# Interleaved memory attention and token-mixing MLP: weights streamed in row blocks over two head groups

## The chip, the cores and the metric

The kernel runs on one core of a Trainium2 chip. The metric is the device time of one execution in microseconds (us), as the median of the runs shown. PE is the matrix engine, DVE the vector engine, ACT the scalar engine, POOL the GpSimd engine; SP issues most of the transfers, and 16 DMA engines carry them out.

## What is computed

Two layers A and B are applied in turn, twice, each on a layer norm of x (2048 tokens, 640 features, bf16) and with a residual. A is an attention with a recurrent memory, cut to what matters:

```python
mem = mem0                                     # 8 rows of 640
for s in range(64):                            # segments of 32 tokens
    h = concat([mem, x[32*s:32*s+32]])         # 40 rows
    q, k, v = h @ Wq, h @ Wk, h @ Wv           # 32 heads of 192: weights 640 x 6144 each
    p = softmax(where(mask, q @ k.T * scale, -1e9))
    o = (p @ v) @ Wo                           # 6144 x 640
    mem = o[:8]; outs.append(o[8:])            # the next segment needs this one's memory
```

B is a token mixer and an MLP: `h = gelu(layernorm(x) @ w1)`, then the four quarters of the 640 features of h are shifted by +1, -1, +2 and -2 tokens, `x1 = x + shifted @ w2`, and the result is `x1 + gelu(layernorm(x1) @ w3) @ w4` with 1536 inner features.

## The kernel before

**Steps and lanes.** The recurrence makes A serial in its segments. The kernel runs the first A layer (lane 0) and the second (lane 1, five segments behind, `LAG`) side by side: one call of `attention_step(t)` computes segment t of lane 0 and segment t - 5 of lane 1, 2 x 40 = 80 columns. There are 69 steps; the first five and the last five have one lane only (40 columns). Every step needs all weights of A (4 x 7.86 MB), which do not fit on the chip, so a part stays resident and the rest is streamed again in every step.

**Attention.** Heads go in 8 groups of 4 (`HG`). `proj(g)` computes keys and queries feature-major (weights stationary, the 80 columns of `hT` moving, L503, 30 matmuls each) and copies them to `kT` (DVE) and `qT` (ACT). Values are made token-major (the columns of `hT` stationary, 384 weight columns moving, L535, two halves of 5 matmuls) and copied by ACT (L540). `attend(g)` has scores (L558), mask and minimum (L569), four exponentials, one a head, each with its row sum (L577), the reciprocal (L582) and the product (L583) on DVE, transposes of the probabilities (L591) and their copy (L596), the product with the values (L605), its copy `oT` (L611), and the output product into `psy` (L623). The output products of the last three groups are due at the step's end (`OT_BUFS` is 4). `psy` gives the memory columns of the next step's `hT` (L640), on which all of its projections wait.

**Weights.** Each of the four weights has 8 x 2 units of half a group; a unit of Wq, Wk or Wv is 640 x 384, loaded by one DMA with rows of 768 B, a unit of Wo 384 x 640 with rows of 1280 B; both are 480 KB. Of 64 units `N_RES` = 37 are resident and 27 are streamed in each step through a ring of `RING_A` = 5 slots (tile `wst`, L427).

**Mixer.** Every second step a chunk of 128 rows (64 tokens of both lanes) goes through B in `chunk` and `chunk_end`: transposes (`psx` L783), layer norms, w1 (L873), `gelu`, w2 (L896), w3 in four parts (L928), `gelu`, w4 (L948), and the normalised result (`psn`) goes into lane 1's `hT` (L982). The memory of lane 0's tokens is thus ready some two steps later, which `LAG` covers. Its weights are streamed for each chunk in 12 loads through a ring of `RING_B` = 1 slot (tile `wstB`, `load_b`); w1 comes from a copy `w1d` in device memory that is reordered at the start, and the second load of w2 is five DMAs (L457, L460).

**Order.** Every operation is added to a `Plan` with its engine, a planned duration, a due time (`STEP` = 48 us per step) and the buffers that it reads and writes. `place()` then plays the program through once with these costs and a simple model of the DMAs, and the order that results on each engine is the program. Loads of the two rings are two queues ("wa", "wb"), each in order of due time, and both are issued by SP:

```python
srv = max(s + 1.6, srv) + o.dma / DMA_RATE
done = srv + 0.4
```

PSUM has 8 banks: one for `psy`, three for projections ("P"), two for attention ("S"), two for the mixer ("B").

## Time and profile before

| | |
|---|---|
| median of 3 runs | 4157.51 us (4153.1 to 4164.62) |
| span of the profiled execution | 4200.0 us |
| PE busy | 3679.9 us (88%) |
| DVE busy | 2221.0 us (53%) |
| ACT busy | 1960.1 us (47%) |
| moved by DMA | 1154.32 MB, mean 275 GB/s |

The profiled execution is one of its own and a little longer than the median. Busy times overlap, and matmuls are pipelined, so PE's busy time is an upper reading of its work. A wait is the idle time of an engine ahead of an instruction, put down to what released it; "DMA wstB" is the landing of a load into that tile. The clock is the share of TensorE's 2.4 GHz that was granted; it has two levels, 0.5 and 1.0.

### The profile page before, as it was taken

To read this page: it belongs to the slowest core of one execution; us is meant where nothing else is said; L and a number is where in the kernel's file an instruction comes from. 1 tells how busy PE (TensorE), PEld (TensorE's weight loads), DVE (VectorE), ACT (ScalarE), POOL (GpSimd) and SP (SyncE) were. 2 spreads that over 40 slices of the span, in tenths; PEclk is the share of its full clock that TensorE was granted. 3 is DMA by queue.
4 is the path that set the end of the run, shared out by engine and by line. 5 is a ranking of instruction groups with operands and counts; after the bars stand their busy time and mean duration, and the time that the engine had idled before them with its cause. 6 is when DMAs were issued, how large, how long until landed. Compare 5 with 4: busy or idle time off the path is not lost.

```text
span 4200.0 us, 162257 instructions
## 1 busy us (share of the span) xinstructions
PE 3679.9 (88%) x70351; PEld 3232.6 (77%) x70351; DVE 2221.0 (53%) x6403; ACT 1960.1 (47%) x7380; POOL 280.8 (7%) x489
## 2 busy tenths in 40 slices
PE   6998888889899898989898989888989888989993
PEld 4777877888888787878887888787878777877771
DVE  2455555555555555555555555555545555555452
ACT  2444444444454444544444544444544444445440
POOL 1000000000000000000000000000000000000000
PEclk7999999999999999999999999999999999999995
DMA  9998888888898888988888888888888888889992
GB/s 360 300 312 280 266 267 274 276 281 267 269 289 274 267 277 275 284 273 276 279 271 271 279 273 275 278 263 274 276 254 279 273 275 278 268 280 289 318 298 78
DMA packets 1365962, 1154.32 MB, mean 275 GB/s; under 512 B 44094, under 2 KB 1362380, under 8 KB 1365248
## 3 DMA queue, kind: packets, MB, share of 16 engines
q1 hardware_dynamic: 1357536, 1129.19, 86.0%
q0 software_dynamic: 7712, 14.76, 1.0%
q8 instruction: 552, 9.04, 0.8%
q14 instruction: 162, 1.33, 0.1%
HBM read 1137.72 MB, written 6.06 MB: 272 GB/s over the span
## 4 chain that ended last, share of the span: by engine, by line
PE 67%; DMA 25%; issue 2%; SPq 2%; ACT 2%; DVE 1%; POOL 0%; ACTq 0%; POOLq 0%; DVEq 0%
DMA wstB<-in_B_w_dram 19%; PE psv L535 16%; PE psk L503 13%; PE psq L503 12%; PE psy L623 8%; DMA wstB<-w1d 4%; PE psh L928 3%; PE y L948 3%; PE pso L605 3%; PE pss L558 3%; PE pst L591 2%; PE psh L873 1%; PE hs L896 1%; SPq L460 1%; ACT Pm L577 1%
## 5 line engine op out<-in xcount | busy, mean ns | idle before, releaser
L577 ACT ACTIVATE Pm<-pss,sm 80x80 bf16<-80x80 f32 (+1 forms) x2208 | 673.3, 314 | 186.8 <-DVE sm L569 186.2
L540 ACT CAST V<-psv 80x384 bf16<-80x384 f32 (+1 forms) x1104 | 522.1, 474 | 507.4 <-PE psv L535 504.2
L535 PEld LDWEIGHTS <-hT 128*80 128x80 bf16 (+1 forms) x5520 | 586.4, 117 | 213.7 <-issue 15.8
L503 PEld LDWEIGHTS <-wst 128*128 128x128 bf16 x14490 | 611.3, 103 | 24.8 <-issue 5.9
L535 PE MATMUL psv<-wv,hT 128*80 128x384 bf16 (+1 forms) x3105 | 611.5, 332 | 2.3 <-DMA wv<-in_A_Wv_dram 2.1
L611 DVE CAST oT<-pso 128x480 bf16<-128x480 f32 (+1 forms) x552 | 342.3, 620 | 412.9 <-PE pso L605 411.5
L510 ACT CAST qT<-psq 128x480 bf16<-128x480 f32 (+1 forms) x552 | 292.1, 529 | 504.4 <-PE psq L503 493.9
L535 PE MATMUL psv<-wst,hT 128*80 128x384 bf16 (+1 forms) x2415 | 483.6, 332 | 0.7 <-DMA wst<-in_A_Wv_dram 0.4
L503 PE MATMUL psk<-hT,wk 128*128 128x80 bf16 (+1 forms) x9315 | 441.8, 205 | 17.6 <-ACT hT L640 13.0
L623 PE MATMUL psy<-oT,wo 128*128 128x80 bf16 (+1 forms) x10350 | 454.1, 200 | 2.2 <-DVE oT L611 1.5
L503 PE MATMUL psq<-hT,wq 128*128 128x80 bf16 (+1 forms) x9315 | 440.5, 203 | 5.8 <-DMA wq<-in_A_Wq_dram 5.7
L577 ACT ACTIVATION_READ_ACCUMULATOR Pm<-pss,sm 80x1 f32 (+1 forms) x2208 | 437.0, 198 | 0.0
L503 PEld LDWEIGHTS <-wk 128*128 128x128 bf16 x9315 | 396.8, 104 | 40.4 <-issue 22.2
L569 DVE CUSTOM_DVE_ANT_1 pss<-pss,mask 80x320 f32<-80x320 f32 x472 | 232.8, 493 | 358.5 <-PE pss L558 357.8
L623 PEld LDWEIGHTS <-wo 128*128 128x128 bf16 x10350 | 402.1, 100 | 14.7 <-issue 7.9
L596 ACT COPY PT<-pst 80x320 bf16<-80x320 bf16 (+1 forms) x552 | 221.5, 401 | 369.1 <-PE pst L591 365.3
L518 DVE CAST kT<-psk 128x320 bf16<-128x320 f32 (+1 forms) x552 | 256.3, 464 | 246.5 <-PE psk L503 243.6
L503 PEld LDWEIGHTS <-wq 128*128 128x128 bf16 x9315 | 379.0, 102 | 7.2 <-DMA wq<-in_A_Wq_dram 6.7
L503 PE MATMUL psk<-hT,wst 128*128 128x80 bf16 (+1 forms) x7245 | 357.1, 206 | 2.7 <-DMA wst<-in_A_Wk_dram 2.6
L503 PE MATMUL psq<-hT,wst 128*128 128x80 bf16 (+1 forms) x7245 | 342.4, 203 | 4.4 <-DMA wst<-in_A_Wq_dram 4.4
L524 DVE CAST kT<-psk 64x160 bf16<-64x160 f32 (+1 forms) x1104 | 336.7, 305 | 8.3
L623 PE MATMUL psy<-oT,wst 128*128 128x80 bf16 (+1 forms) x6210 | 284.0, 199 | 53.0 <-DVE oT L611 52.0
(114 smaller groups left out, 4193.2 us busy)
## 6 DMA issues: line engine op xcount, KB each, us to landing
wst<-in_A_Wk_dram SPq DMA_DIRECT2D x483, 480.0 KB, 5.3
wst<-in_A_Wq_dram SPq DMA_DIRECT2D x483, 480.0 KB, 5.5
wst<-in_A_Wv_dram SPq DMA_DIRECT2D x483, 480.0 KB, 5.2
wst<-in_A_Wo_dram SPq DMA_DIRECT2D x414, 480.0 KB, 5.5
wstB<-in_B_w_dram SPq DMA_DIRECT2D x315, 480.0 KB, 4.8
wstB<-w1d SPq DMA_DIRECT2D x35, 480.0 KB, 4.8
wstB<-w1d SPq DMA_DIRECT2D x35, 320.0 KB, 5.2
wstB<-in_B_w_dram SPq DMA_DIRECT2D x35, 160.0 KB, 3.8
```

The costliest lines, as they stand in the source:

```text
L503: nc.tensor.matmul(out=o[:, hf * GCH + cc, 0:N], lhsT=w[:, kc, cc * P:(cc + 1) * P], rhs=h[:, kc, c0:c0 + N], start=(kc == 0), stop=(kc == ...
L510: nc.scalar.copy(out=q[:, :, 0:N], in_=T(pq)[:, :, 0:N])
L518: nc.vector.tensor_copy(out=k4[:, :, 0::3, 0:N], in_=p4[:, :, 0::2, 0:N])
L524: nc.vector.tensor_copy(out=k4[r0:r1, :, j, 0:N], in_=p4[r0:r1, :, 1, 0:N])
L535: nc.tensor.matmul(out=o[0:N, :], lhsT=h[:, kc, c0:c0 + N], rhs=w[:, kc, :], start=(kc == 0), stop=(kc == KC - 1))
L540: nc.scalar.copy(out=v_runs(V_, hf)[0:N], in_=T(pv)[0:N, :].rearrange("n (a b) -> n a b", a=2))
L558: nc.tensor.matmul(out=o[0:N, i * N:(i + w_) * N].rearrange("p (a b) -> p a b", a=w_), lhsT=q[:, c, 0:N], rhs=k_[:, j:j + w_, 0:N], start= ...
L569: nc.vector.tensor_tensor_reduce(out=o, in0=o, in1=maskt[:].unsqueeze(1).to_broadcast([N, HG, N]), scale=-scale, scalar=3.0e38, op0=ALU.ad ...
L577: nc.scalar.activation(out=Pb[0:N, i, 0:N], in_=o[0:N, i * N:(i + 1) * N], func=ACT.Exp, bias=sm_[0:N, 0:1], scale=-1.0, accum_out=sm_[0:N ...
L596: nc.scalar.copy(out=Pt[0:N, :, 0:N], in_=T(pst)[0:N, :, 0:N])
L611: nc.vector.tensor_copy(out=o_[:, :, 0:N], in_=T(pso)[:, :, 0:N])
L623: nc.tensor.matmul(out=o[:, m, c0:c0 + N], lhsT=w[:, cc, m * P:(m + 1) * P], rhs=o_[:, hf * GCH + cc, 0:N], start=st, stop=True, skip_grou ...
```

## The change

- **Row blocks over two groups.** `proj_pair(pr)` takes two head groups at once. A streamed block is 128 rows of Wk, Wq or Wv by 1536 columns (3 KB of each row, 384 KB), and both groups use it. Of the five row blocks of each weight, three are streamed for keys and queries and two for values (`STREAM`); the others are resident. That makes 8 streamed blocks per pair, 32 per step, in a ring of 7 slots of 384 KB. Each group's projection is cut into one operation for the resident rows and one for each streamed block.
- **Wo resident.** All of Wo stays on the chip. Output products of four groups, not three, are due at the step's end.
- **Values feature-major.** Values are computed like keys and queries (30 matmuls a group), copied to `vF` (ACT), transposed on PE (6 a group, `pvt`), and copied to `V` in two halves, one on ACT and one on DVE. `V` has two buffers, not three.
- **Softmax.** One exponential over the four heads, without row sums; DVE adds them up (`tensor_reduce`).
- **Mixer.** w1 and w3 are loaded by rows (w3 in two column halves), at most two row blocks to a load: 3 + 3 + 6 + 6 = 18 loads per chunk in two slots of 384 KB. All output columns of w1, or of half of w3, collect in the two banks at once, and their `gelu`s follow. `w1d` is gone, w2 is loaded in plain rows, and the token shift is made as `gelu` writes `hTB`, in nine pieces, not six.
- **Shared buffers.** `vx` and `xo` are now `vb`; `uw`, `vx2` and `h2T` share `h2u`; there is one `gl`. Projections and attention share one pool of 5 PSUM banks ("A").
- **Planner.** Planned DMA costs are other ones: 380 GB/s, 0.37 us to issue, 2.0 us of latency.

```diff
 HG = 4
-N_RES = 37
-RING_A = 5
-RING_B = 1
+STREAM = {"k": 3, "q": 3, "v": 2}
+RING_A = 7
+RING_B = 2
 STEP = 48.0
-PSUM_POOLS = {"y": 1, "P": 3, "S": 2, "B": 2}
-OT_BUFS = 4
-V_BUFS = 3
+PSUM_POOLS = {"y": 1, "A": 5, "B": 2}
+OT_BUFS = 5
 LAT = 0.2
 PE_LAT = 0.25
-DMA_RATE = 350.0e3
+DMA_RATE = 380.0e3
+DMA_ISSUE = 0.37
+DMA_LAT = 2.0
+LEAD_A = 0.0
+LEAD_B = 0.0
 
...
             cand[e].remove(o)
             out.append(o)
             left -= 1
@@ -246,11 +249,11 @@
...
-    uw = ctile([XB, Dm], f32, "uw")
+    h2u = ctile([P, FC * XB], bf16, "h2u")
+    uw = h2u[:, 0:2 * Dm].bitcast(f32)
+    vx2 = h2u[:, 0:Dm]
+    h2T = h2u[:].rearrange("p (c n) -> p c n", c=FC)
...
+    vx = vb
+    xo = vb
...
-    gl = [ctile([P, 3 * XB], f32, f"gl{i}") for i in range(2)]
+    gl = ctile([P, 3 * XB], f32, "gl")
...
+    ALIAS = {("vx",): ("vb",), ("xo",): ("vb",), ("vx2",): ("uw",)}
...
+    def load_pair(kind, pr, due, now):
+
+        nres = KC - STREAM[kind]
+        cols = slice(PW * pr, PW * (pr + 1))
+        rb, rt = res_tile((kind, pr), [P, nres, PW], w_src[kind][:, 0:nres, cols], due)
+        slots = []
+        for j, kc in enumerate(range(nres, KC)):
+            b = Slotted("ra", None)
+            b.make = lambda b=b: wring.tile([P, SLOT], bf16, name="wst", tag=f"ra{b.slot}")
+
+            def fn(op, b=b, kc=kc):
+                nc.sync.dma_start(out=T(b)[:, 0:PW], in_=w_src[kind][:, kc, cols])
+            add("SP", DMA_ISSUE, due - now + 0.01 * j, fn, w=(b,), dma=2 * P * PW, queue="wa")
+            slots.append(b)
+
+        def view(kc, c0, c1):
+            if kc < nres:
+                return rt[:, kc, c0:c1]
+            return T(slots[kc - nres])[:, c0:c1]
+        return (rb, *slots), view
...
+    def load_b(nm, a, e, due, half=0):
...
+        W = GW if nm == "w3" else Dm
...
-            t = T(b)
...
             if nm == "w1":
-                nc.sync.dma_start(out=v, in_=w1d[:, :, a * P:e * P])
+                nc.sync.dma_start(out=v, in_=w1_v[:, a:e, :])
             elif nm == "w3":
-                nc.sync.dma_start(out=v, in_=w3_v[:, :, a * P:e * P])
+                nc.sync.dma_start(out=v, in_=w3_v[:, a:e, GW * half:GW * (half + 1)])
             elif nm == "w4":
...
-                    for gi in range(4):
-                        nc.sync.dma_start(out=v[32 * gi:32 * gi + 32, 4 - a, :], in_=src[P:QD, gi, :])
-        add("SP", 0.06 if nm != "w2" or e <= 4 else 0.3, due, fn, r=rd, w=(b,), dma=P * n * Dm * 2, queue="wb")
+                nc.sync.dma_start(out=v, in_=w2_v[:, a:e, :])
+        add("SP", DMA_ISSUE, due - LEAD_B, fn, w=(b,), dma=P * n * W * 2, queue="wb")
...
-                        k4 = k_[:].rearrange("p (h c) n -> p h c n", h=2)
-                        nc.vector.tensor_copy(out=k4[:, :, 0::3, 0:N], in_=p4[:, :, 0::2, 0:N])
-                    add("DVE", dve_us(4 * N), s0 + off, fk, r=(pq,), w=(B("kT", G % 2, 0),))
-                    for part, (r0, r1, j) in enumerate(((0, 64, 1), (64, P, 2))):
-                        def fk2(op, pq=pq, k_=k_, r0=r0, r1=r1, j=j):
+        def proj_pair(pr):
+            s0 = base + sl * 2 * pr
+            for kind, off in (("k", 0.0), ("q", 0.2), ("v", 0.5)):
+                wbs, wv = load_pair(kind, pr, s0 + off * 2 * sl, LEAD_A)
+                for j in range(2):
+                    g = 2 * pr + j
+                    G = t * NG + g
+                    due = s0 + (off + 0.1 * j) * 2 * sl
+                    pq = ps("A", [P, GC, NS], f32, "ps" + kind)
+
+                    nres = KC - STREAM[kind]
+                    for kcs in [range(0, nres)] + [range(kc, kc + 1) for kc in range(nres, KC)]:
+                        def fn(op, pq=pq, wv=wv, j=j, kcs=kcs):
+                            o = T(pq)
+                            for cc in range(GC):
+                                for kc in kcs:
+                                    nc.tensor.matmul(out=o[:, cc, 0:N],
+                                                     lhsT=wv(kc, GW * j + cc * P, GW * j + (cc + 1) * P),
+                                                     rhs=h[:, kc, c0:c0 + N], start=(kc == 0 and cc == 0),
...
-                                         start=(kc == 0), stop=(kc == KC - 1))
-                add("PE", mm_us(GWH, k=KC), due, fv, r=(wb, *hk), w=(pv,))
-
-                def fe(op, pv=pv, V_=V_, hf=hf):
-                    nc.scalar.copy(out=v_runs(V_, hf)[0:N], in_=T(pv)[0:N, :].rearrange("n (a b) -> n a b", a=2))
-                add("ACT", act_us(GWH), due, fe, r=(pv,), w=(B("V", G % V_BUFS, hf),))
+                            nc.vector.tensor_copy(out=k4[:, :, 0::3, 0:N], in_=p4[:, :, 0::2, 0:N])
+                        add("DVE", dve_us(4 * N), due, fk, r=(pq,), w=(B("kT", G % 2, 0),))
+                        for part, (r0, r1, jj) in enumerate(((0, 64, 1), (64, P, 2))):
+                            def fk2(op, pq=pq, k_=k_, r0=r0, r1=r1, jj=jj):
+                                p4 = T(pq)[:].rearrange("p (h c) n -> p h c n", h=2)
+                                k4 = k_[:].rearrange("p (h c) n -> p h c n", h=2)
+                                nc.vector.tensor_copy(out=k4[r0:r1, :, jj, 0:N], in_=p4[r0:r1, :, 1, 0:N])
+                            add("DVE", dve_us(2 * N), due, fk2, r=(pq,), w=(B("kT", G % 2, 1 + part),))
+                    else:
+                        vf, V_ = vF, Vt[G % 2]
+
+                        def fvf(op, pq=pq, vf=vf):
+                            nc.scalar.copy(out=vf[:, :, 0:N], in_=T(pq)[:, :, 0:N])
+                        add("ACT", act_us(GC * N), due, fvf, r=(pq,), w=(B("vF"),))
+                        pvt = ps("A", [NS, GW], bf16, "pvt")
+
+                        def fvt(op, pvt=pvt, vf=vf):
+                            o = T(pvt)
+                            for c in range(GC):
+                                nc.tensor.transpose(out=o[0:N, c * P:(c + 1) * P], in_=vf[:, c, 0:N], identity=ident[:, :])
+                        add("PE", mm_us(P, k=GC), due + 0.1 * sl, fvt, r=(B("vF"),), w=(pvt,))
+                        for hf in range(2):
+                            def fe(op, pvt=pvt, V_=V_, hf=hf):
...
+                o = T(pss)[0:N, 0:HG * N].rearrange("p (a b) -> p a b", a=HG)
+                nc.scalar.activation(out=Pb[0:N, :, 0:N], in_=o, func=ACT.Exp, bias=sm_[0:N, 0:1], scale=-1.0)
+            add("ACT", act_us(HG * N), hi - 4, f2, r=(pss, smk), w=(Pk,))
 
             def f3(op):
+                nc.vector.tensor_reduce(out=sm_[0:N, 4:4 + HG], in_=Pb[0:N, :, 0:N], axis=AX.X, op=ALU.add)
...
+            add("DVE", 0.42 + 0.17 + 0.45, hi - 4, f3, w=(Pk, B("sm4", G % 4)))
+            pst = ps("A", [NS, HG, NS], bf16, "pst")
...
             add("DVE", dve_us(GC * N), hi - 4, f7, r=(pso,), w=(B("oT", G % OT_BUFS),))
+            due = base + STEP - 1 + 0.02 * g if g >= NG - OT_BUFS + 1 else s0 + 2.0 * sl
+            wb, wo = res_tile(("o", g), [P, GC, Dm], Wo_v[:, g], s0 + 1.2 * sl)
...
+        for pr in range(NPAIR):
+            proj_pair(pr)
+            attend(2 * pr)
+            attend(2 * pr + 1)
...
+        gk = B("gl")
...
+        pz = [ps("B", [P, 3, XB], f32, "psh") for _ in range(2)]
+        for i, (a, e) in enumerate(((0, 2), (2, 4), (4, KC))):
+            due = D(0.2 + 0.05 * i)
+            wb, wv = load_b("w1", a, e, due)
+
+            def fw(op, a=a, e=e, wv=wv):
+                w = wv()
+                for kc in range(a, e):
+                    for n in range(KC):
+                        nc.tensor.matmul(out=T(pz[n // 3])[:, n % 3, :], lhsT=w[:, kc - a, n * P:(n + 1) * P],
+                                         rhs=vT[:, kc, 4:XB + 4],
+                                         start=(kc == 0 and n % 3 == 0), stop=(kc == KC - 1), skip_group_check=True)
+            add("PE", mm_us(128, k=KC * (e - a)), due, fw, r=(wb, vTk, B("vTl")), a=tuple(pz))
...
+                    r = r1
+            gelu(pz[i], e - a, due, outs, (B("hTB", i),))
         hs = [ps("B", [XB, HC], f32, "hs") for _ in range(2)]
-        for i, (a, e) in enumerate(((0, 3), (3, 5))):
+        for i, (a, e) in enumerate(((0, 2), (2, 4), (4, 5))):
             due = D(0.4 + 0.1 * i)
...
-                                         rhs=vT[:, kc, 0:XB], start=(kc == 0), stop=(kc == KC - 1))
-            add("PE", mm_us(128, k=KC * (e - a)), due, fw, r=(wb, vTk), w=(pz,))
-            gelu(pz, 3, i % 2, due, [(0, P, 0, 3, h2T[:, a:e, :])], (B("h2T", i),))
+        for half in range(2):
+            pz2 = [ps("B", [P, 3, XB], f32, "psh2") for _ in range(2)]
+            for i, (a, e) in enumerate(((0, 2), (2, 4), (4, KC))):
+                due = D(0.75 + 0.3 * half + 0.05 * i)
+                wb, wv = load_b("w3", a, e, due, half)
+
+                def fw(op, a=a, e=e, wv=wv, pz2=pz2):
+                    w = wv()
...
+                                             rhs=vT[:, kc, 0:XB], start=(kc == 0 and n % 3 == 0), stop=(kc == KC - 1),
+                                             skip_group_check=True)
+                add("PE", mm_us(128, k=6 * (e - a)), due, fw, r=(wb, vTk), a=tuple(pz2))
...
+                gelu(pz2[i], 3, D(0.9 + 0.3 * half + 0.05 * i),
+                     [(0, P, 0, 3, h2T[:, 6 * half + 3 * i:6 * half + 3 * i + 3, :])], (B("h2T", 2 * half + i),), (uk,))
...
+        for i in range(6):
+            a, e = 2 * i, 2 * i + 2
+            due = D(1.3 + 0.06 * i)

```

## Rows read from the trace of the kernel before

**Rows 1.** The page's heading: span of the profiled execution.
```profile
span 4200.0 us, 162257 instructions
```
**Rows 2.** Windows: length; busy PE, PEld, DVE, ACT, POOL; clock, DMA share, GB/s.
```profile
302.00:3835.00 3533.00, 3161.11 (x60067) 2840.16 (x60063) 1945.47 (x5441) 1702.71 (x6306) 226.94 (x377) 0.95 0.88 274
...
3835.00:4041.00 206.00, 187.41 (x4078) 146.38 (x4076) 103.71 (x367) 99.51 (x423) 15.28 (x27) 0.98 0.99 316
4041.00:4200.00 159.00, 80.92 (x1232) 58.70 (x1231) 53.55 (x160) 35.45 (x126) 9.84 (x18) 0.66 0.47 142
```
**Rows 3.** Marks of a step's end (L640) in 300:3840: first and last start.
```profile
L640 ACT CAST hT<-psy x60: 192/225/226, 302.2 to 3835.2; 128x80 bf16<-128x80 f32 x58, 128x40 bf16<-128x40 f32 x2
```
**Rows 4.** Waits of PE in 302:3835: us in total, times, longest.
```profile
PE y L948 <- DMA wstB<-in_B_w_dram: 90.3, 57, 3.3
PE psh L928 <- DMA wstB<-in_B_w_dram: 68.9, 31, 3.3
PE hs L896 <- DMA wstB<-in_B_w_dram: 56.2, 57, 2.1
PE psy L623 <- DVE oT L611: 47.6, 59, 0.9
PE psh L873 <- DMA wstB<-w1d: 44.6, 29, 2.5
PE pso L605 <- ACT PT L596: 39.9, 59, 0.8
PE pst L591 <- DVE Pm L583: 14.6, 30, 1.0
PE psk L503 <- ACT hT L640: 9.4, 30, 0.3
PE psk L503 <- DMA wst<-in_A_Wk_dram: 0.2, 1, 0.2
```
**Rows 5.** Waits of the SP queue in 302:3835, the longest in total.
```profile
SPq L427 <- PE psk L503: 405.5, 314, 3.4
```
**Rows 6.** DMA issues in 302:3835: times, KB each, us to landing.
```profile
wst<-in_A_Wq_dram SPq DMA_DIRECT2D x414, 480.0 KB, 5.4
...
wstB<-in_B_w_dram SPq DMA_DIRECT2D x265, 480.0 KB, 4.7
```
**Rows 7.** Chain of waits, a full step: start us, us, what.
```profile
2011.80 0.28 PE psn L691 x5
...
2012.61 1.07 PE psq L503 x30
2013.69 1.63 PE psv L535 x10
...
2034.72 0.28 PE psx L783 x5
...
2086.28 5.95 DMA wstB<-in_B_w_dram
```
**Rows 8.** Windows: the stretch behind that wait.
```profile
2092.28:2095.50 3.22, 3.22 (x40) 3.22 (x41) 0.72 (x2) 0.49 (x1) 0.00 (x0) 0.50 0.18 42
```
**Rows 9.** DMA in 0:100: packets and mean rate.
```profile
DMA packets 42278, 36.34 MB, mean 363 GB/s; under 512 B 1350, under 2 KB 41914, under 8 KB 42266
```
**Rows 10.** ACT groups by form in 302:3835: busy us, mean ns.
```profile
L577 ACT ACTIVATE Pm<-pss,sm 80x80 bf16<-80x80 f32 x1888 | 584.8, 319 | 144.4 <-DVE sm L569 144.4
...
L596 ACT COPY PT<-pst 80x320 bf16<-80x320 bf16 x472 | 198.8, 421 | 337.0 <-PE pst L591 333.3
```
**Rows 11.** DVE groups by form in 302:3835.
```profile
L583 DVE TENSOR_TENSOR Pm<-Pm,sm 80x320 bf16<-80x320 bf16 x472 | 230.0, 487 | 16.1
```
**Rows 12.** Chain of waits in a single-lane step.
```profile
147.29 0.75 PE psq L503 x30
148.05 1.73 PE psv L535 x10
```
**Rows 13.** Chain of waits at the end, the last chunk.
```profile
4105.79 3.33 DMA wstB<-in_B_w_dram
```

## The prediction, made blind

> **What bounds the kernel now.** I read the windows first, then the step marks, then the waits of TensorE and of the SP queue, then the DMA issues, and last the chain for durations. The profiled execution spans 4200.0 us [rows 1]; the median of the runs is 4157.51 us, 0.990 of it, so I sum against 4200.0 and scale at the end. The three runs lie within 0.28% of each other, so 0.3% is about what can be told from no change.

> Of the span, 3533 us are 59 full steps of two lanes, 59.88 us each [rows 2, 3]. In them PE is busy for 3161 us, DVE for 1945, ACT for 1703, and the DMA engines show 0.88 at 274 GB/s [rows 2]. A busy share of 0.88 looks like a DMA bound, but the waits say otherwise. The waits of PE add up to 371.7 us (3533.0 less 3161.1 is 371.9). Of them, 260.0 us (90.3 + 68.9 + 56.2 + 44.6, in 174 waits of 1.49 us on average) are matmuls of the mixer that wait for wstB; 111.5 us (47.6 + 39.9 + 14.6 + 9.4) are the end of each step, where the last head group runs through softmax alone; and a streamed attention weight was late once, by 0.2 us [rows 4]. The attention ring is so far ahead that SP stands waiting for PE to free its slots: the largest of those waits alone is 405.5 us [rows 5]. So attention streaming sets nothing. What sets the time is PE's own work, plus a mixer ring with one slot: the next load can only be issued when the matmuls of the one before are done, and it lands 4.7 us later [rows 6].

> A third loss hides inside "busy": the mean granted clock is 0.95 of 2.4 GHz [rows 2]. After a chain wait of 5.95 us for wstB, PE works at 0.50, which is the 1.2 GHz level, for 3.2 us [rows 7, 8]. Over the 3533 us the missing 0.05 is 177 us of clock; some of it lies in idle time, so at most its busy share, 177 x 3161/3533 = 158 us, is lost work.

> **Packets and bytes.** An attention load was 5 x 128 packets of 768 B and becomes 128 of 3 KB. I give the packet size itself nothing: in the first 100 us, with loads queued deep, 42278 packets of on average 860 B already moved at 363 GB/s [rows 9]. Per step the streamed bytes go from 27 units of 491,520 B (13.27 MB) to 32 blocks of 393,216 B (12.58 MB); the mixer keeps 5.57 MB per chunk of two steps, 2.79 MB per step. Together 16.06 becomes 15.37 MB: 285 GB/s at the step of 54 us that I arrive at, against 274 now and 363 shown. The first step loads 31.46 MB in both (18.19 resident + 13.27 streamed, or 18.87 + 12.58), so the start costs the same: 0.

> **Values, feature-major.** Removed per full step: 16 projections of 5 matmuls, two of which take 1.63 us [rows 7], so 8 x 1.63 = 13.04 us. Added: 240 matmuls of the form of q, 30 of which take 1.07 us, so 8.56 us; and 48 transposes, at 0.28 us per five of the 128-column form of psx [rows 7] 2.69 us. Net -1.79 us per step, x 59 = **-106 us**. Accumulating in another order (by block, six columns at a time) adds nothing that I can see: the instructions keep their form.

> By those rows a weight load and its matmul take 36 ns together at 80 columns and 56 ns at 128, which is what the sum uses. [...]

> **Mixer loads.** The 12 loads per chunk become 18 smaller ones in two slots (w2's last block was five DMAs and is one; w1d goes). A load can be issued when the matmuls two loads back are done. Today's chain from psx to psn takes two steps less 2034.72 - 2011.80 = 22.9 us [rows 7], so 96.9 us, or 8.1 us per load. With 18 loads a turn is 5.4 us and a load starts two turns ahead, 10.8 us instead of 8.1: 2.7 us earlier, more than the mean wait of 1.49. But the order of PE was planned with an assumed landing time, so some matmuls will still come just ahead of their data. Bounds: all of it goes (-260), or each of 18 loads waits as each of 12 does now (+130). I take **-160 us**, leaving 100. The clock follows those waits: bounds 0 and -158, taken **-80 us**.

> **Softmax, V copies, end of the step.** Four activations of 319 ns become one, like the 80 x 320 copy of 421 ns; a row sum is added on DVE, at most the 487 ns of the 80 x 320 product [rows 10, 11]. That shortens the last group's chain by about 0.37 us. The V path grows by a copy and six transposes, but is off that chain while the output products of four deferred groups (three before) cover it. Bounds per step -0.5 and +1.0 us; taken -0.34, **-20 us**. DVE gains 8 x (0.487 + a V half of about the same) = 7.8 us on 33.0 per step: 40.8 of 54, hidden behind PE; ACT loses work.

> **Attention ring.** It goes to 7 slots, for 8 blocks per pair of groups, and a block serves both groups, so its slot is held longer. Bounds 0 and +88 us (one late block per step at 1.49 us); taken **+20 us**. SP issues loads in one order: a mixer load that waits for its slot holds up the attention loads behind it; that is where such a wait would come from.

> **Single-lane steps and the end.** Eight steps run one lane, four of them in a window of 206 us [rows 2], 51.5 us each. There values cost 8 x 1.73 = 13.84 us [rows 12] and will cost 8 x 0.75 + 2.69 = 8.69, so PE could gain 5.15 us; but DMA already shows 0.99 at 316 GB/s there [rows 2], and 15.37 MB needs 48.6 us at that rate, 42.3 at 363. Bounds 0 and -41; taken 3.5 us a step, **-28 us**. The end, 159 us with PE busy for 80.9 at clock 0.66 [rows 2], is the last mixer chunk with nothing beside it, waiting some 3.33 us per load [rows 13]: 12 x 3.33 = 40 us. Two slots hide part: **-25 us**, bounds 0 and -40.

> **Sum.** -106 - 160 - 80 - 20 + 20 - 28 - 25 = -399 us. A full step becomes 54.0 us, the span 3801 us; x 0.990 = **3763 us**, 9.5% faster.

> **Rivals.**
> A, the mixer waits vanish and the clock stays at 1.0. For it: two slots, and loads for the next stage that can land during the GELUs. Against it: the planned landing time. -106 - 260 - 158 - 20 + 20 - 41 - 40 = -605: 3559 us.
> B, the waits stay: DMA takes the 18 loads as late as the 12. For it: the ring is full and loads queue behind attention blocks (5.4 us to land for an attention block) [rows 6]. Only -106 - 20 + 20 - 28 - 25 = -159 is left: 4000 us.
> C, slower: the mixer's chain outgrows two steps. vb, vx and xo now share one tile, uw, vx2 and h2T another, there is one gl, and both psh banks finish only after the last block, so two GELUs run one after the other where one ran beside the next load. Two rows of chunk c's result must stand in hT when step 2c+4 begins, two steps after the chunk does. The chain takes 96.9 of 119.8 us now; it must grow past 119.8 to cost anything. Were the 6 further loads all exposed at 4.7 us, it would take 125.1: +5.3 us per two steps, x 29.5 = +156, and the kernel, less the 53 us of the single-lane steps and the end, ends at 4260 us.
> D, slower: weight loads of the new values are not hidden behind matmuls. If a pair took 71 ns, twice the row's 36, values would cost 17.1 + 2.7 - 13.0 = +6.8 us a step instead of -1.8: -399 + 106 + 400 = +107, or 4263 us. Nothing in the rows speaks for it. [...]

> **How the numbers follow.** The forecast (3640 to 3920) 0.60; A 0.13; B 0.15, of which 0.02 reach no change; C 0.09; D 0.01; anything else near no change 0.02, half of it within 0.3% and half slower. So faster 0.86 (0.60 + 0.13 + 0.13), same 0.03, slower 0.11. The range from 3540 to 4040 us leaves out 0.04 of A, 0.04 of B, and C, D and the rest, about 0.2.

> **What would show it.** PE waits for wstB in the full steps near 100 us instead of 260, for attention blocks near 20; a mean clock of 0.97 to 0.98 there; step marks 54.0 us apart; 30 value matmuls in 1.07 us and six transposes in 0.34; DMA near 285 GB/s with a lower busy share. Wrong: PE waiting for wst blocks or for hT's columns out of psn (L982) at the start of even steps (B, C), waits on DVE that grow by more than 1 us a step, or waits for wstB of 260 us or more.

## The result and the profile after

The changed kernel takes 3980.06 us (median of four runs, 3963.16 to 3996.05) against 4159.64 us for the kernel before, run beside it: a ratio of 0.956, with a 95% interval from 0.953 to 0.960. It is 4.4% faster, where 9.5% was forecast. That lies inside the range of 3540 to 4040 us, but outside the forecast's own 3640 to 3920, and close to the 4000 us of rival B.

The profiled execution spans 3969.8 us. Windows of the kernel after (columns as in [rows 2]): four single-lane steps at the start, the 59 full steps, four single-lane steps, the end.

```profile
92.90:292.50 199.60, 176.04 (x4851) 157.89 (x4851) 116.52 (x422) 68.39 (x197) 11.96 (x21) 0.93 0.88 302
292.50:3622.10 3329.60, 3001.45 (x72348) 2894.60 (x72345) 2284.67 (x6475) 1367.56 (x3005) 213.84 (x377) 0.99 0.81 279
3622.10:3826.40 204.30, 180.24 (x4906) 159.25 (x4906) 123.09 (x437) 69.27 (x199) 15.12 (x27) 0.94 0.88 306
3826.40:3969.80 143.40, 80.27 (x1440) 62.08 (x1439) 59.61 (x182) 28.52 (x71) 9.74 (x18) 0.67 0.46 144
```

A full step takes 56.43 us (3329.6 / 59), down from 59.88 [rows 2, 3]; 54.0 was forecast. PE is busy for 160 us less and idle for 328 us where it was idle for 372. The waits of PE in the full steps (us in total, times, longest) show what is left:

```profile
PE psh L933 <- DMA wstB<-in_B_w_dram: 69.4, 51, 3.9
PE psh L873 <- DMA wstB<-in_B_w_dram: 55.3, 29, 3.1
PE y L956 <- DMA wstB<-in_B_w_dram: 45.9, 34, 2.9
PE hs L901 <- DMA wstB<-in_B_w_dram: 39.8, 29, 2.2
PE psk L495 <- ACT hT L640: 37.0, 57, 1.0
PE psq L495 <- DMA wst<-in_A_Wq_dram: 21.8, 35, 1.3
PE psk L495 <- DMA wst<-in_A_Wk_dram: 15.9, 27, 1.6
PE psy L622 <- issue: 8.9, 16, 1.1
```

The first four rows are the mixer's weights: 210.4 us in 143 waits, against 260.0 in 174 [rows 4]. The second slot and the smaller loads took 50 us off, not 160. Attention weights, late once before, now cost 39.2 us. The end of the step is shorter: its softmax waits, three rows of 102.1 us before [rows 4], have nearly gone, and 45.8 us of waits on ACT and DVE are left in all, most of them on the next step's `hT` (37.0). The last row is of a kind that the kernel before does not have: PE waits for nothing that the profile shows ("issue"), 24.0 us over all its rows.

The SP queue's longest wait and two DMA issues of the full steps (times, KB each, us to landing) answer to [rows 5, 6]:

```profile
SPq L420 <- PE psk L495: 915.3, 240, 9.4
```
```profile
wst<-in_A_Wq_dram SPq DMA_DIRECT2D x708, 384.0 KB, 5.9
wstB<-in_B_w_dram SPq DMA_DIRECT2D x298, 320.0 KB, 5.4
```

A mixer load is a third smaller and lands later, after 5.4 us where it was 4.7 (medians of the commonest size). Rows from the chain of waits in a full step (start, us, what) answer to [rows 7]:

```profile
1931.16 1.08 PE psq L495 x30
...
1942.51 5.29 DMA wstB<-in_B_w_dram
...
1954.26 0.34 PE pvt L532 x6
1954.60 0.22 PE psv L495 x6
1954.82 1.07 PE psk L495 x30
```

Thirty pairs still take 1.07 us and six transposes 0.34, as forecast. On ACT and DVE (busy us, mean ns), the single exponential takes 525 ns where four took 319 each; the row sum and the V copies are the work that came to DVE:

```profile
L577 ACT ACTIVATE Pm<-pss,sm 80x320 bf16<-80x320 f32 x472 | 247.9, 525 | 106.4 <-DVE sm L570 103.9
L581 DVE TENSOR_REDUCE sm<-Pm 80x4 f32<-80x320 bf16 x472 | 224.6, 476 | 6.3 <-ACT Pm L577 5.3
L538 DVE COPY V<-pvt 80x384 bf16<-80x384 bf16 x472 | 162.6, 349 | 182.3 <-ACT V L540 111.4 <-PE pvt L532 67.4
```

### The profile page after: what moved, and what is told of

Read it like the earlier page. It is cut to its first block, busy times and chain, and to the rows that moved or that the text cites. A ratio compares the mean times of both kernels' runs of the same rounds, so it can differ in the third digit from the quotient of the medians.

```text
span 3969.8 us, 187915 instructions
## 1 busy us (share of the span) xinstructions
PE 3493.2 (88%) x84703; PEld 3320.3 (84%) x84703; DVE 2608.1 (66%) x7611; ACT 1550.0 (39%) x3516; POOL 257.6 (6%) x467
## 4 chain that ended last, share of the span: by engine, by line
PE 59%; DMA 34%; issue 2%; ACT 2%; DVE 2%; SPq 0%; POOL 0%; POOLq 0%; ACTq 0%; DVEq 0%
DMA wstB<-in_B_w_dram 21%; PE psy L622 12%; PE psk L495 11%; PE psv L495 10%; PE psq L495 8%; DMA wst<-in_A_Wq_dram 7%; PE pvt L532 3%; DMA wst<-in_A_Wk_dram 3%; PE pss L559 3%; PE y L956 3%; PE pso L605 3%; PE psh L933 2%; PE pst L591 2%; DMA wst<-in_A_Wv_dram 1%; PE hs L901 1%
## 5 line engine op out<-in xcount | busy, mean ns | idle before, releaser
L495 PEld LDWEIGHTS <-wst 128*128 128x128 bf16 x26496 | 1076.6, 100 | 94.8 <-DMA wst<-in_A_Wq_dram 37.9
L622 PE MATMUL psy<-oT,wo 128*128 128x80 bf16 (+1 forms) x16560 | 713.5, 201 | 34.1 <-issue 14.2
L570 DVE CUSTOM_DVE_ANT_1 pss<-pss,mask 80x320 f32<-80x320 f32 (+1 forms) x512 | 246.0, 480 | 487.0 <-PE pss L559 429.3
L495 PE MATMUL psv<-hT,wv 128*128 128x80 bf16 (+1 forms) x9936 | 442.9, 201 | 11.2 <-DMA wv<-in_A_Wv_dram 6.6
L525 ACT CAST vF<-psv 128x480 bf16<-128x480 f32 (+1 forms) x552 | 291.4, 528 | 286.5 <-PE psv L495 281.3
L495 PEld LDWEIGHTS <-wv 128*128 128x128 bf16 x9936 | 391.7, 101 | 12.9 <-DMA wv<-in_A_Wv_dram 7.3
L540 ACT COPY V<-pvt 80x384 bf16<-80x384 bf16 (+1 forms) x552 | 262.4, 475 | 304.3 <-PE pvt L532 255.7
L495 PE MATMUL psk<-hT,wk 128*128 128x80 bf16 (+1 forms) x6624 | 320.6, 199 | 45.8 <-ACT hT L640 40.0
L495 PE MATMUL psv<-hT,wst 128*128 128x80 bf16 (+1 forms) x6624 | 352.1, 201 | 7.0 <-DMA wst<-in_A_Wv_dram 6.2
L577 ACT ACTIVATE Pm<-pss,sm 80x320 bf16<-80x320 f32 (+1 forms) x552 | 278.4, 505 | 141.4 <-DVE sm L570 138.9
L532 PE MATMUL pvt<-ident,vF 128*80 128x128 bf16 (+1 forms) x3312 | 286.7, 224 | 2.7 <-issue 1.2
```

The source lines that it names most:

```text
L495: nc.tensor.matmul(out=o[:, cc, 0:N], lhsT=wv(kc, GW * j + cc * P, GW * j + (cc + 1) * P), rhs=h[:, kc, c0:c0 + N], start=(kc == 0 and cc ...
L525: nc.scalar.copy(out=vf[:, :, 0:N], in_=T(pq)[:, :, 0:N])
L532: nc.tensor.transpose(out=o[0:N, c * P:(c + 1) * P], in_=vf[:, c, 0:N], identity=ident[:, :])
L540: nc.scalar.copy(out=v_runs(V_, hf)[0:N], in_=src)
L570: nc.vector.tensor_tensor_reduce(out=o, in0=o, in1=maskt.unsqueeze(1).to_broadcast([N, HG, N]), scale=-scale, scalar=3.0e38, op0=ALU.add, ...
L577: nc.scalar.activation(out=Pb[0:N, :, 0:N], in_=o, func=ACT.Exp, bias=sm_[0:N, 0:1], scale=-1.0)
```

## The theories

**P, the plan.** PE runs its matmuls in the order that the planner wrote down. With nothing ahead of it, the planner of the changed kernel lets a 320 KB load land 0.8 + 0.86 + 1.2 = 2.9 us after its issue; with loads ahead it adds their transfer. Over the 530 mixer loads of the full steps that makes 4.1 us on average, and the trace has 5.3. The planner before assumed 1.6 + 1.4 + 0.4 = 3.4 us for 480 KB with nothing ahead, 3.75 on average, and the trace has 5.0. So a matmul that the plan puts right behind its load comes too early. The text below calls a load "without slack" when its first matmul stands less than 1 us behind its planned landing.

**The rivals.** Q: the landing time grows with the bytes that are outstanding in the queues, and the mixer waits because it shares them with deeper attention loads. F: a landing costs a fixed time, whatever the bytes. S, slots: the mixer's ring is still too short. For the "issue" waits, theory I: feature-major values are many short weight loads and matmuls, and PE runs out of instructions.

Sums of PE's waits over the full steps, in us, worked out from the rows of each run; "mixer" is wstB, "attention" is wst:

```
run                     ratio   step   PE busy clock  mixer  attention issue  other
before                  1       59.88  3161.1  0.95   260.0     0.2     0.0  111.5
after                   0.9563  56.43  3001.5  0.99   210.4    39.2    24.0   45.8
c1_replan               0.9421  55.72  2987.6  0.99   178.5    51.9    28.0   34.4
c2_half_bytes           0.8556  50.90  2927.2  1.00    22.5     0.3     0.2   44.9
c3_plan_late            0.9054  53.15  2966.3  1.00    10.3    23.8    50.6   78.8
c4_three_slots          0.9248  54.79  2996.7  0.99    19.9   151.3    28.4   21.2
d1_before_plan_late     0.9327  54.93  3075.2  0.98    31.5     6.6     0.9  125.1
d2_before_values        1.0136  59.82  3087.7  0.96   264.3    10.2    37.4  128.2
d3_plan_later           0.9264  54.40  3008.5  0.99     0.0     0.3    57.1  133.9
d4_late_three_slots     0.9062  53.49  2973.1  1.00     0.0    20.0    83.1   73.2
f1_late_mixer_only      0.9069  53.36  2958.4  1.00     8.8    67.6    62.1   45.8
f2_late_attention_only  0.9435  55.83  2988.3  0.99   158.7     7.5    63.7   72.4
f3_late_old_softmax     0.9167  53.79  2968.5  1.00     8.9    11.6    55.0  115.4
f4_late_old_values      0.8904  52.57  3012.7  1.00    11.6     9.5     2.4   59.4
g1_split_values         0.9172  53.96  3060.1  1.00     6.1    14.0    34.3   63.5
g2_values_three_slots   0.8881  52.51  3020.5  1.00     6.1    23.6     1.4   42.6
```

The 95% intervals of the ratios reach 0.003 to 0.005 to either side.

The next table sets plan against trace. Playing `place()` through again gives each load's planned landing and the place of its matmuls in PE's order, which is the order of the trace. "Landed" and "PE there" are means over the loads without slack, in us from the issue in the trace: until the data were there, and until PE had reached the first matmul that needs them. Up to one load in seven has no landing on record and is left out of "landed"; sums differ from the table above by rounding.

```
                     mixer  without        of those without slack          waits of
run                  loads  slack    planned  landed  PE there  waits us   the others
before               353    178      3.68     5.42    4.13      259.0      1.1
after                530    205      3.95     5.32    4.37      210.4      0.0
c2_half_bytes        530    205      3.95     3.63    3.97       22.5      0.0
c3_plan_late         531    237      5.68     5.24    5.85       10.2      0.0
c4_three_slots       530     30      5.49     6.57    6.03       19.9      0.0
d1_before_plan_late  354    325      5.96     5.52    6.14       31.5      0.0
```

Where PE is there before the data, it waits; the loads with slack hardly ever make it wait, since PE reaches theirs 12 us after the issue before the change and 15.5 us after it. Three ways out appear in the rows: data that land sooner (c2), matmuls that stand later (c3, d1), and fewer loads without slack (c4).

## The experiments

**Another order for no reason (c1).** One planned latency is moved by 0.01 us.

```diff
-LAT = 0.2
+LAT = 0.21
```

> A control: the changed kernel with one planned cost moved a little (the semaphore delay in the planner from 0.20 to 0.21 us), so that only the order on the engines is drawn anew. All theories: within 0.5% of the changed kernel (3980 us), mixer waits in the full steps near its 210 us. If it moves by more, differences of that size in the runs beside it say nothing.

It took 3940.99 us, 1.0% less than the changed kernel by the medians and 1.5% less by the ratios, more than the 0.5% that was expected. This is the yardstick: an edit that makes the planner write another order can move the time by that much, so smaller differences between two orders are not put down to the edit. It is one such order; how far others would scatter was not tried.

**Half the bytes (c2).** A streamed attention block brings only the columns of the first of its two groups, and both groups compute with them: the second group's streamed rows are the wrong ones, and the work and the order on PE are unchanged.

```diff
-nc.sync.dma_start(out=T(b)[:, 0:PW], in_=w_src[kind][:, kc, cols])
+nc.sync.dma_start(out=T(b)[:, 0:GW], in_=w_src[kind][:, kc, GW * 2 * pr:GW * (2 * pr + 1)])
...
-            return T(slots[kc - nres])[:, c0:c1]
+            return T(slots[kc - nres])[:, c0 % GW:c0 % GW + c1 - c0]
```

> The changed kernel in its own order, but each streamed attention block brings 768 of its 1536 columns and both head groups of a pair compute with these (the output is another one); number, order and slots of the loads stay. Theory Q (mixer loads land late because they queue behind the bytes of attention blocks): landing of the 320 KB mixer loads falls from 5.4 to about 4 us, mixer waits from 210 to under 80 us, time about 3840 us. Rival F (a fixed time per load and the number of loads in flight set the landing, not bytes): landing stays above 5 us, waits near 210, time within 1% of 3980 us.

3577.25 us, a ratio of 0.856. Its window of the full steps, the mixer's waits and its loads:

```profile
254.40:3257.50 3003.10, 2927.23 (x72348) 2846.06 (x72347) 2273.60 (x6475) 1369.13 (x3004) 213.48 (x377) 1.00 0.62 186
```
```profile
PE psh L933 <- DMA wstB<-in_B_w_dram: 8.0, 15, 1.0
...
PE y L956 <- DMA wstB<-in_B_w_dram: 5.6, 9, 1.2
PE psh L873 <- DMA wstB<-in_B_w_dram: 5.2, 10, 1.1
PE hs L901 <- DMA wstB<-in_B_w_dram: 3.7, 9, 0.9
```
```profile
wstB<-in_B_w_dram SPq DMA_DIRECT2D x298, 320.0 KB, 4.0
```

The mixer's own loads are the same, yet land after 4.0 us and not 5.4, and their waits fall to 22.5 us. So the landing time is not fixed (F falls), and Q is right about what makes it long. With the landing now at the planner's 4.1 us, the unchanged order fits. In the trace of the changed kernel the mixer's landing, counted from the end of the issue and as a mean over loads of 160 to 384 KB, goes with the number of loads still outstanding on SP's queue; there were 3.0 ahead of a mixer load on average, and 2.3 in the kernel before:

```
loads outstanding    0     1     2     3     4     5
loads               28    22    83   172   114    45
us to landing     2.78  3.08  4.06  4.91  5.47  6.88
```

The bytes count beside the number: behind three loads c2 has 3.79 us, behind four 4.35.

**A later plan (c3).** Only the latency that the planner assumes is changed; the program's loads, slots and sizes stay.

```diff
-DMA_LAT = 2.0
+DMA_LAT = 4.0
```

> The changed kernel with the planner's DMA latency at 4.0 us instead of 2.0, so that it places the matmuls of a load some 2 us later behind its issue; hardware work is the same. Theory P (the waits are there because the order was planned with too short a landing time): mixer waits fall from 210 to under 100 us, those for attention blocks from 39 to under 15, time about 3880 us. Theory Q alone (the queue itself is too slow for the mixer's chain): waits move elsewhere or stay, time within 1% of 3980 us or longer, as the mixer's chain stretches.

3786.18 us, a ratio of 0.905. The window, the mixer's waits and its loads:

```profile
298.20:3434.30 3136.10, 2966.28 (x72354) 2861.74 (x72353) 2296.57 (x6481) 1358.45 (x3008) 214.22 (x377) 1.00 0.86 296
```
```profile
PE psh L933 <- DMA wstB<-in_B_w_dram: 3.9, 8, 0.8
...
PE psh L873 <- DMA wstB<-in_B_w_dram: 3.2, 6, 0.8
...
PE y L956 <- DMA wstB<-in_B_w_dram: 2.6, 8, 0.7
...
PE hs L901 <- DMA wstB<-in_B_w_dram: 0.6, 1, 0.6
```
```profile
wstB<-in_B_w_dram SPq DMA_DIRECT2D x298, 320.0 KB, 5.6
```

The loads land no sooner, 5.6 us, and the waits are gone, 210.4 to 10.3 us, while DMA moves more, 296 GB/s. So neither bandwidth nor landing time as such set the mixer's waits, but the place of the matmuls in the order: PE now reaches those without slack 5.85 us after the issue. Waits for attention blocks stay at 23.8 us, where under 15 were expected.

**A third slot (c4).** The attention ring gives one slot to the mixer.

```diff
-RING_A = 7
-RING_B = 2
+RING_A = 6
+RING_B = 3
```

> The changed kernel with the same nine slots cut 6 + 3 instead of 7 + 2: three slots for the mixer's loads. Theory S (two slots are too few to hide a landing): mixer waits fall from 210 to under 110 us, time about 3890 us, unless the attention ring at 6 slots waits. Theories P and Q: mixer waits fall by less than a third, and waits for attention blocks grow from 39 us; time within 1.5% of 3980 us.

3866.21 us, a ratio of 0.925, 3.3% faster than the changed kernel. P's forecast failed here: it said that the mixer's waits would fall by less than a third, and they fell to 19.9 us, as S said. The plan shows why: with three slots it issues loads so early that 30 of 530 are left without slack. The price is waits for attention weights, of which these are the largest rows, and one row of the mixer's is left:

```profile
PE psk L495 <- DMA wst<-in_A_Wk_dram: 72.6, 132, 1.9
PE psv L495 <- DMA wst<-in_A_Wv_dram: 40.2, 51, 2.2
PE psq L495 <- DMA wst<-in_A_Wq_dram: 38.5, 78, 1.4
PE y L956 <- DMA wstB<-in_B_w_dram: 19.9, 22, 2.8
```

**The later plan without the change (d1).** The kernel before, with 2.0 us more of planned latency.

```diff
-done = srv + 0.4
+done = srv + 2.4
```

> The kernel before with one planned cost changed: a load is planned to land 2.0 us later. Theory P (the order planned with too short a landing time makes the mixer waits, in either kernel): mixer waits fall from 260 to under 100 us, the clock rises with them, time about 3950 us, as fast as the changed kernel. Rival R (with one slot the loads are serial whatever the order; the second slot is needed): waits stay above 180 us or the mixer's chain outgrows its two steps, time within 1.5% of the kernel before.

3893.42 us, a ratio of 0.933: one number in the planner of the kernel before is worth more than the whole change. With one slot, a planned landing of 5.4 us with nothing ahead (6.0 on average) and a measured one of 5.5, the mixer waits for 31.5 us and not 260.0, so the second slot was not needed for that:

```profile
290.00:3530.60 3240.60, 3075.22 (x60076) 2762.80 (x60077) 1933.53 (x5444) 1727.21 (x6310) 234.00 (x377) 0.98 0.95 299
```
```profile
PE y L948 <- DMA wstB<-in_B_w_dram: 12.8, 26, 1.1
...
PE hs L896 <- DMA wstB<-in_B_w_dram: 9.1, 23, 0.7
PE psh L873 <- DMA wstB<-w1d: 6.8, 9, 1.4
```

**Feature-major values alone (d2).** The values' part is put into the kernel before.

```diff
-                pv = ps("P", [NS, GWH], f32, "psv")
+            pq = ps("P", [P, GC, NS], f32, "psv")
...
+                    for cc in range(GCH):
+                        for kc in range(KC):
+                            nc.tensor.matmul(out=o[:, hf * GCH + cc, 0:N], lhsT=w[:, kc, cc * P:(cc + 1) * P],
+                                             rhs=h[:, kc, c0:c0 + N], start=(kc == 0), stop=(kc == KC - 1))
...
+                    nc.tensor.transpose(out=o[0:N, c * P:(c + 1) * P], in_=vF[:, c, 0:N], identity=ident[:, :])
```

> The kernel before with one part of the change: values feature-major, copied to vF, transposed, copied in two halves. By the forecast's term: PE work 1.8 us less per full step and up to 5 us per single-lane step, so -106 and about -28 us, 4040 us, 3% faster. Rival W (waits of the order take it up): under 1% faster although 30 value matmuls take 1.07 us and six transposes 0.34. A new order alone moved the changed kernel by 1%, so only a difference beyond that counts.

4232.86 us, a ratio of 1.014. PE is busy for 73 us less in the full steps, and the step is as long as before, 59.82 us: what the matmuls gave came back as waits, 37.4 us of them without a releaser. The 1.4% itself is within what another order does.

**Later still, and late with a third slot (d3, d4).** In d3 `DMA_LAT` is 6.0; d4 is c3 with the slots of c4.

```diff
-DMA_LAT = 2.0
+DMA_LAT = 6.0
```

> The changed kernel with the planner's DMA latency at 6.0 us (2.0 in the change, 4.0 in the run before). Theory P: beyond the real landing of about 5.4 us there is nothing left to win from the mixer (its waits are under 30 us already), and the plan now holds slots too long; time within 1% of the 3786 us at 4.0. Rival: if latency was not yet covered at 4.0, waits for attention blocks (18.6 us for queries) vanish too and time falls below 3745 us.

```diff
-RING_A = 7
-RING_B = 2
+RING_A = 6
+RING_B = 3
...
-DMA_LAT = 2.0
+DMA_LAT = 4.0
```

> The changed kernel with the planner's latency at 4.0 us and the slots cut 6 + 3. Theory P: the order was the cause, so the third slot adds nothing on top: within 1% of 3786 us, with waits for attention blocks as the six slots' price. Theory S: slots and order add up, time below 3720 us.

d3 took 3870.55 us (0.926), 2.2% more than c3 where at most 1% was expected: hardly a wait for weights is left, but the waits on ACT and DVE grow to 133.9 us, so the plan can also be too late. d4 took 3785.88 us (0.906), as c3: with a plan that fits, the third slot adds nothing. Slots and plan are two ways to the same end.

**Which queue's latency (f1, f2).** The 2.0 us are added for the mixer's loads alone ("wb"), and for the attention's alone ("wa" in its place).

```diff
-done = srv + DMA_LAT - 0.8
+done = srv + DMA_LAT - 0.8 + (2.0 if in_queue.get(o.i, ("",))[0] == "wb" else 0.0)
```

> The changed kernel with 2.0 us more planned latency for the mixer's loads alone. Theory P (it is the place of the mixer's matmuls in PE's order that was planned too early): mixer waits fall from 210 to under 90 us, waits for attention blocks stay near 39 us or grow, time at or below 3850 us, most of the way to the 3786 us of all loads. Rival A (the attention loads' plan did it): above 3920 us.

> The changed kernel with 2.0 us more planned latency for the attention loads alone. Theory P: mixer waits stay above 150 us, time between 3900 and 3990 us. Rival A: below 3850 us.

f1 took 3798.8 us (0.907), all of c3's gain within 0.2%; f2 took 3950.69 us (0.944), within what another order does, and its mixer still waits for 158.7 us. It is the mixer's plan.

**The softmax and the values of before, under the late plan (f3, f4).** Both start from c3. f3 takes back the four exponentials with their row sums, f4 the token-major values.

```diff
-                nc.scalar.activation(out=Pb[0:N, :, 0:N], in_=o, func=ACT.Exp, bias=sm_[0:N, 0:1], scale=-1.0)
...
+                for i in range(HG):
+                    nc.scalar.activation(out=Pb[0:N, i, 0:N], in_=o[0:N, i * N:(i + 1) * N], func=ACT.Exp,
+                                         bias=sm_[0:N, 0:1], scale=-1.0, accum_out=sm_[0:N, 4 + i:5 + i])
...
-                nc.vector.tensor_reduce(out=sm_[0:N, 4:4 + HG], in_=Pb[0:N, :, 0:N], axis=AX.X, op=ALU.add)
```

> The changed kernel with the planner's latency at 4.0 us and the softmax of before (an exponential per head with its row sum, no sum on DVE). The forecast's term of 0.34 us per step: 20 us slower than 3786. Rival D (DVE is what the change loads, and the old form relieves it): up to 1.5% faster. A new order alone can move it by 1%.

```diff
+                        pvs = [ps("A", [NS, GWH], f32, "psv") for _ in range(2)]
...
+                                        c = GW * j + GWH * hf
+                                        nc.tensor.matmul(out=o[0:N, :], lhsT=h[:, kc, c0:c0 + N], rhs=wv(kc, c, c + GWH),
+                                                         start=(kc == 0), stop=(kc == KC - 1))
```

> The changed kernel with the planner's latency at 4.0 us and token-major values as before (two halves of 5 matmuls of 384 columns, both halves copied by ACT, no transposes). The forecast's term: 1.8 us more PE work per full step, 106 us and about 28 in the single-lane steps, so 3860 to 3920 us against 3786. Rival W (as in the kernel before, where this part alone made it 1.4% slower): at or below 3786 us.

f3 took 3830.02 us (0.917). The sign is the forecast one and the waits on ACT and DVE grow by 37 us, but 1.2% is within what another order does. f4 took 3727.57 us (0.890), 1.7% less than c3. Counted from start to start of PE's instructions, the value matmuls and transposes take 13.41 us of a step in f4 and 11.81 in c3, so feature-major is 1.6 us shorter by itself. But PE's busy time is only 0.8 us a step shorter in c3, its waits are 1.4 us longer (the "issue" rows alone 0.8), and a single-lane step takes 50.4 to 51.3 us against 46.9 to 49.2.

**The short pairs without the copies (g1).** f4, with every value matmul of 384 columns cut into four of 96: more pairs of weight load and matmul, the same products, copies and order.

```diff
-                                        nc.tensor.matmul(out=o[0:N, :], lhsT=h[:, kc, c0:c0 + N], rhs=wv(kc, c, c + GWH),
-                                                         start=(kc == 0), stop=(kc == KC - 1))
+                                        for u in range(4):
+                                            nc.tensor.matmul(out=o[0:N, 96 * u:96 * u + 96], lhsT=h[:, kc, c0:c0 + N],
+                                                             rhs=wv(kc, c + 96 * u, c + 96 * u + 96),
+                                                             start=(kc == 0 and u == 0), stop=(kc == KC - 1),
+                                                             skip_group_check=True)
```

> The kernel of late plan and token-major values (3728 us), in the same order, with each value matmul of 384 columns cut into four of 96: 320 pairs of weight load and matmul per step where there were 80, the same columns, and no copies, transposes or DVE work added. By the columns alone it costs some 0.6 us per step, 35 us. Theory I (PE runs out of instructions when it works through many short pairs): waits of PE that nothing releases come back from 3 us to over 40 us, and the short matmuls beside them slow from 36.2 towards 37 ns; time 3790 us or more. Theory V (what feature-major values lose comes from their copies and waits on ACT and DVE): no such waits, time at most 3770 us.

3836.54 us (0.917): 2.9% slower than f4. The "issue" waits are back, 34.3 us where f4 has 2.4, a little under what was expected, and the single-lane steps take 50.6 and 52.6 us. That the matmuls beside them get slower, as theory I had it, was not shown. Its largest "issue" rows and the packets that carry instructions (packets, MB, share), first those of g1, then of f4:

```profile
PE psv L498 <- issue: 11.3, 19, 1.6
...
PE psy L645 <- issue: 7.7, 15, 1.1
...
PE pst L614 <- issue: 6.3, 8, 1.3
...
q8 instruction: 679, 11.12, 1.2%
```
```profile
q8 instruction: 550, 9.01, 1.0%
```

The number of these packets goes with PE's instructions. There are 662 of 16 KB after the change, for 169591 instructions of PE in the trace (weight loads, matmuls and under 200 others), and 552 before, for 141449: 256.2 to a packet in both. That they carry PE's instructions, 64 bytes each and 256 to a packet, is an estimate from these counts. With it the waits can be tested one by one: ahead of each, how many instructions had PE started, beyond 256 for each packet that was in before the one that came last?

```
run                   issue gaps over 0.2 us   instructions started beyond the packets
                                               at these gaps     at all other gaps
after                 38                       449 at each       201 to 655
c3_plan_late          77                       449 at each       194 to 624
d4_late_three_slots  107                       449 at each       241 to 655
g1_split_values       57                       449 at each       238 to 628
f4_late_old_values     3                       449 at each       247 to 643
c2_half_bytes          0                       -                 199 to 505
before                 0                       -                 193 to 590
```

By this count every one of the 282 gaps stands at the same instruction of a packet. At all 2746 such places in the five runs with gaps, PE started that instruction no sooner than 1.2 us after the packet's end, and the waits stand where that time was 1.2 to 1.64 us (elsewhere it was 3.1 us in the median after the change). That is what theory I forecast: by the count, PE stood until the next packet was in. How PE takes its instructions from a packet was not shown. The gaps also went with busy DMA engines: c2 has the instructions of the changed kernel, with the engines at 0.62 and 186 GB/s, and not one such gap. Busy engines alone did not bring many: d1, at 0.95 with the fewer instructions of the kernel before, has two "issue" waits, 0.9 us together.

**The best version (g2).** f4 with the slots of c4.

```diff
-RING_A = 7
-RING_B = 2
+RING_A = 6
+RING_B = 3
```

> The kernel of late plan and token-major values (3728 us) with the slots cut 6 + 3. Theory P: mixer waits are already under 15 us there, so the third slot can help only at the end, where one chunk runs alone (20 us, as in the runs with three slots before); time 3700 to 3730 us. If two slots were still short, below 3690 us.

3709.32 us, a ratio of 0.888 (0.884 to 0.892): 11.2% faster than before. Against f4 the intervals overlap, so the third slot is not shown to add anything. The gain is that of row blocks, resident Wo, smaller mixer loads, the single exponential and the late plan, with the values as they were.

## Why the prediction went wrong

**The step that failed is the mixer's.** The prediction said: "a load starts two turns ahead, 10.8 us instead of 8.1: 2.7 us earlier, more than the mean wait of 1.49." From this it took -160 us. The term measured -50, and 110 of the 169 us by which the span of 3801 was missed are here. The 2.7 us came true as an average: from a load's issue to its first matmul the plan has 10.6 us where it had 7.9, and the trace has 11.2 where it had 8.1. What failed is to set an average lead against an average wait. Before, all but 1.1 us of the waits stood at the 178 loads without slack; after, all of them stand at 205 such loads. At these PE comes 4.37 us after the issue where it came 4.13, and they land after 5.32 where they landed after 5.42. The gain went to loads that had not waited. The prediction's next sentence named the cause ("some matmuls will still come just ahead of their data") and left 100 us for it without counting these matmuls; the planner's landing could have been set beside the 4.7 and 5.4 us of the trace [rows 6].

Rival B, the waits stay, came nearer with 4000 us, in part by luck: its reason, loads queued behind attention blocks, is what c2 shows for the landing time, but it left out 50 us of the mixer's gain, 81 of the clock and 46 at the end of the step, and what the other terms fell short of made up for most of that.

**Clock: right in size by luck, not in reason.** The low clock was to follow the mixer's waits. PE's busy time in the full steps fell by 160 us, of which 79 are the value matmuls, so 81 are left against a forecast of 80. In the records of the granted clock, which have the two values 0.5 and 1.0, the full steps spend 331 us at 0.5 before, in 74 stretches, and 99 us after, in 28, although the mixer's waits fell by 50 us only. In the trace before, matmuls of 384 columns (L535) start 163 ns apart at 1.0 and 320 ns at 0.5, those of 128 columns (L928) 56 and 107 ns, in the median. That is 2.4 and 1.2 further columns per ns, which the prediction calls 2.4 and 1.2 GHz. PE is busy for 289 us of the low stretches before and 96 of those after; had that work run at 1.0 and taken half the time, as an estimate from these spacings, it would have saved 145 and 48 us, which makes the fall worth at most 97. What fell is the number of PE's gaps over 2 us, from 55 to 31, and the waits at the end of the step. d1 has 113 us at the low clock and no gap over 1.5 us, so those gaps are not all of it; which waits bring the low clock was not tried.

**Values: the matmuls right, the sum not.** The term was -1.79 us a step; by start times they gave 1.34 (13.47 to 12.13). The 36 ns of a pair stayed [rows 7]: the trace after shows 30 pairs of 80 columns in 1.07 us again, 36 ns each, and six of 128 columns in 0.34 us, 57 ns each, so rival D did not happen. What was missed, and put at nothing, is the instruction packets that pairs of 36 ns use up: 24.0 us of "issue" waits after, 50.6 in c3. With the late plan this part of the change costs 1.7%. It gives way to token-major values in the best version. That 1.7% is only just beyond the yardstick of c1, and what lies in it beyond the "issue" waits is not settled: in g1 the extra pairs cost 47 us of busy time and 35 us of waits in the full steps.

**Softmax, V copies, end of the step: more than forecast.** -66 us on the waits on ACT and DVE against -20. By the durations shown, one exponential and the row sum take 1001 ns where four exponentials took 1276, an estimate of 0.28 us a step or 16 us for the softmax itself; how much of it is the softmax is open, since f3 lies within the yardstick of c1.

**Attention ring:** +39 us against +20, well inside its bounds. f2 takes it to 7.5 us with a later plan for these loads alone, and c4 to 151.3 with a slot less; of the 64 waits after the change 32, 20 us of the 39, are for a load that SP issued right behind one of the mixer's, but whether that held them up, as the prediction had it, was not tried.

**Single-lane steps and the end:** about -8 us against -28, and -16 against -25. The windows show DMA at 0.88 in the single-lane steps, where 0.99 was feared as a limit [rows 2]; "issue" waits appear there too, and f4's shorter steps (46.9 to 49.2 us, with the late plan) suggest that the missing part lies with the values.

**The scale.** The profiled execution of before was 1.0% above its median, that of after 0.2% below it (3971.5 us against 3980.06). Scaling by 0.990 took a chance difference for a property of the program. The two differences are worth 48 us of the miss in the median, 38 of them by the scaling.

**What held.** DVE's growth stayed hidden: it is busy for 38.7 us of a step (2284.67 / 59), and 40.8 were forecast. DMA moves 279 GB/s against 285. Neither rival C's chain nor waits on `psn` showed.

**The whole.** The span fell by 230 us: 203 in the full steps, 16 at the end, 8 in the single-lane steps, 3 at the start. By terms, the 169 us of the miss are the mixer's 110, the values' 27, the "issue" waits' 24, 20 of the single-lane steps, 19 of the attention ring and 9 of the end, less 46 for the end of the step, 3 for the start and 1 for the clock; the rest are idle gaps of PE too short to be listed as waits. With both plans late, d1 against c3, the change is worth 2.9% (0.9054 / 0.9327); without its values, d1 against f4, 4.5%. That is close to the 4.4% of the change as it was made, but by another sum: the waits that its second slot was to remove are removed by the plan on both sides.

## What to carry to other kernels

Where an order is planned ahead, set the planner's latency beside the landing times of the trace before counting what slots or packet sizes will bring, and count the loads that the plan leaves without slack: an earlier start was worth nothing to the others here, which cost 1.1 us of waits before and 0.0 after. One constant of the planner can be worth more than a restructuring, as in d1 (0.933, against 0.956 for the change). Before costing many short matmuls by their own duration, count the instruction packets that they use up, one for 128 pairs or 4.6 us here by the estimate below, above all where the DMA engines are as busy as in the runs with gaps (0.81 to 0.87). And run an arbitrary re-plan first, better several, to know how large a difference between two orders means something.

## What the runs showed of the hardware

```profile
DMA packets 16950, 36.70 MB, mean 367 GB/s; under 512 B 1108, under 2 KB 7902, under 8 KB 16938
```
